# One tiled MoE kernel: gating between the decoding operations, a third attention tile moved ahead, a spare accumulator bank

## The chip, the core and the metric

The kernel runs on one core of a Trainium2 chip. The metric is device time in microseconds (us) of one execution, smaller is better. TensorE (PE in the rows, with PEld for its weight loads) does the matmuls and transposes, VectorE (DVE) and ScalarE (ACT) the element-wise work, GpSimd (POOL) the rest, and SyncE's queue (SP, SPq) issues the transfers. Each engine takes its own instructions in the order in which they were written.

## The reference, cut to what matters

Three layers follow each other on 3072 tokens of 512 features:

```
# attention in chunks of 32 rows, over 8 memory rows and a window of 56 keys
a = exp(scale * q_c @ k_full.T - max);  out = (a / sum(a)) @ v_full
# first MoE layer: dense, 512 -> 2048 -> 512
h = x @ w_in;  g = h * clip(h + 3, 0, 6) / 6;  x2 = g @ w_out
# second MoE layer: 8 experts, each token goes to one
idx = argmax(normalised(x2) @ normalised(expert_emb).T / tau)
out[mask] = gate[mask] * (relu(x2[mask] @ w1[e]) @ w2[e])
```

The weights `w_in` and `w_out` arrive in 64 bits a number and are decoded on the chip to a high and a low part of 32 bits each; each product is made of three matmuls (high by high, high by low, low by high).

## The kernel before, in words

Tokens go in 24 tiles of 128. The first dense layer takes them in eight blocks: block 0 of four tiles, block 1 of two, and six blocks of three. Attention of a tile has six stages, `a` (L182: transposes of k and q, then copies into `qT` and `kt`), `s` (L236: scores, `mx`, exponentials), `n` (L269: sums), `p` (L280: transposes of the probabilities, then `pT`), `v` (L294: times v, `xo`; it also issues the transfers of v of the tile after the next) and `x` (L182 again: transposes of `xo` into `xh` and `xl`). They run as side work between the matmuls of an earlier block.

Tiles 0 to 3 are done in a prologue. **Phase one** is the first product of block 0: sixteen steps of twelve matmuls (`mm1`, L393), one for each 128 columns of `w_in`, into two PSUM banks `h` in turn. In each step the engines also decode a later slice of the weights (`decode_w`, L354): three operations on DVE (L369, L370, L371), the second and third waiting for the one before, then a cast on ACT (L376) and a subtraction on POOL (L377); the next slice but two is then requested. Then `gate0` (L426) clamps the step's result: ACT makes relu(h + 3) (L429) and DVE takes the minimum with 6 and multiplies by h (L431), which frees the bank `h` for the step after the next. The last two steps keep their result in the two buffers of the tag `dec`, which the decode also uses. Tile 4 is side work here.

**Phase two** is the second product of block 0 (`mm2`, L449): sixteen steps of twelve matmuls of 512 columns, four tiles at once, with the rest of the decoding (fourteen slices of `w_out`), `split_g` (L437 on ACT, L438 on POOL) and tile 5 as side work. A slice decoded in step t is used in step t + 2.

**Blocks 1 to 7** then run both products in one loop of sixteen steps: `mm1` of step f + 1, side functions of slot f, `mm2` of step f. Side work is attention of the three tiles of the next block and the routing of the block before: `evac` (L457, `x2` from the accumulators), `r_t` (L486: transposes of `x2`, then its split in three by ACT and DVE, L504 to L510), `r_l` (L519: logits), `r_ss`, `r_route`, `r_rank` (L570), `r_sel` (L600), `r_list` (L610), `r_exp`, `r_gate`. Which slot each has is written in tables (`RT4`, `RL4`, tuples in the loop). In block 1 the steps are short, since it has two tiles.

PSUM has eight banks: two for `h`, three for `acc`, two for `s` (stages `a`, `s` and `v`), and one named `att`, which stages `p` and `x` and the routing functions `r_t`, `r_l`, `r_rank` and `r_list` share, one after the other. Block 1 uses two of the three `acc` banks.

The order on each engine is that in which the functions are called here; nothing reorders it. After the three blocks the experts run, which the change does not touch.

Of the kernel before, what the change touches and what calls it, by code (L numbers as in the profile page):

```python
# [30 lines left out]
def attn_moe_kernel(ctx, tc, q, k, v, mem_k, mem_v, w_in, w_out, emb, tau, w1, w2, out, dbg=None):  # L31
# [61 lines left out]
    def bank2():  # L93
        if early["on"]:
            early["s"] += 1
            if early["s"] % 2:
                return pps.tile([P, 2, 512], F32, tag="sp", name="sp", bufs=1)
        return ps.tile([P, 2, 512], F32, tag="s", name="s2", bufs=1)
# [252 lines left out]
            nc.sync.dma_start(out=t.rearrange("p n t -> p (n t)"), in_=w_out[f * P:(f + 1) * P, :])  # L351
        raw[n] = t

    def decode_w(n):  # L354

        f = FORD[n]
        t = raw.pop(n)
        if n < KF:
            t = t.rearrange("p c n t -> p (c n) t")
            dst_h, dst_l = w_in_h[:, :, f * P:(f + 1) * P], w_in_l[:, :, f * P:(f + 1) * P]  # L360
        else:
            for hl in range(2):
                if (hl, f // 2) not in wo:
                    wo[hl, f // 2] = pair(hl, f // 2, F32R)
            dst_h, dst_l = (wo[hl, f // 2][:, f % 2, :] for hl in range(2))
        lo, hi = t[:, :, 0], t[:, :, 1]
        d = late["dw"]().bitcast(I32)
        w = sb.tile([P, 512], I32, tag="dec", name="dec", bufs=2)
        nc.vector.tensor_scalar(out=d, in0=hi, scalar1=0x07FFFFFF, scalar2=3, op0=ALU.bitwise_and, op1=ALU.logical_shift_left)  # L369
        nc.vector.scalar_tensor_tensor(out=d, in0=lo, scalar=29, in1=d, op0=ALU.logical_shift_right, op1=ALU.bitwise_or)  # L370
        nc.vector.scalar_tensor_tensor(out=w, in0=hi, scalar=-0x40000000, in1=d, op0=ALU.bitwise_and, op1=ALU.bitwise_or)  # L371
        load_w(n + 3)
        wf = w.bitcast(F32)
        if n < KF:
            wf = wf.rearrange("p (c n) -> p c n", c=KD)
        nc.scalar.copy(out=dst_h, in_=wf)  # L376
        nc.gpsimd.tensor_tensor(out=dst_l, in0=wf, in1=dst_h.bitcast(F32), op=ALU.subtract)  # L377
# [545 lines left out]
    with tc.manual_schedule():  # L923
# [34 lines left out]

        ndec = [0]

        def dec(n=1):
            for _ in range(n):
                if ndec[0] < 2 * KF:
                    decode_w(ndec[0])
                    ndec[0] += 1

        st = [stages(i) for i in range(BS[0] + BS[1])]
        pw = pps.tile([P, 512], F32, name="pw", bufs=1)
        pdw = pps.tile([P, 512], F32, name="pdw", bufs=1)
        late["dw"] = lambda: pdw  # L970
# [64 lines left out]
        late["ps"] = ctx.enter_context(tc.tile_pool(name="ps2", bufs=1, space=PSUM, reuse_waits="tile"))  # L1035
        late["wp"] = ctx.enter_context(tc.tile_pool(name="wp2", bufs=1, reuse_waits="tile"))
        late["dw"] = lambda: bank("acc", 3)
        a4, a5 = (st[BS[0] + n] for n in range(2))
        side = {1: a4[0], 3: a4[1], 4: a4[2], 6: a4[3], 8: a4[4]}
        hp = mm1(0, 0)  # L1040
        for f in range(KF):
            nxt = mm1(0, f + 1) if f + 1 < KF else None
            if f < KF - 1:
                dec()
            gate0(f, hp)
            if f in side:
                side[f]()
            hp = nxt
# [2 lines left out]
        split_g(1, nc.vector)  # L1051
        pdw2 = bank("h", 2)
        late["dw"] = lambda: pdw2
        side = {0: a5[0], 2: a5[1], 3: a5[2], 5: a5[3], 7: a5[4], 9: a5[5]}
        for t in range(KF):
            mm2(0, STEP[t], first=STEP[0], last=STEP[-1])
            if t + 2 < KF:
                split_g(t + 2)
            dec()
            if t in side:  # L1060
                side[t]()
        for bl in range(NB):
            slot, pre_ = {}, {}
            if bl == 0:
                continue
            if bl + 1 < NB:
                for a in range(TB):
                    st = stages(F0[bl + 1] + a)
                    for o, f_ in zip((0, 1, 2, 3, 4, 5), st):
                        slot.setdefault(5 * a + o, []).insert(0, f_)  # L1070
            if bl:
                d = 2 if bl == 1 else 0
                for t in range(BS[bl - 1]):
                    (wt, f), (wl, f2) = (RT4 if bl == 1 else RT)[t], (RL4 if bl == 1 else RL)[t]
                    (pre_, slot)[wt].setdefault(f, []).append(lambda t=t: r_t(bl - 1, t, bank2()[:, 0, :] if bl == NB - 1 else None))
                    (pre_, slot)[wl].setdefault(f2, []).insert(0, lambda t=t: r_l(bl - 1, t))
                    slot.setdefault((8, 8, 9, 9)[t] + d // 2, []).append(lambda t=t: r_ss(bl - 1, t))
                slot.setdefault(8 + d, []).append(lambda: r_route(bl - 1))
                slot.setdefault(9 + d, []).append(lambda: r_rank(bl - 1))
                slot.setdefault(10 + d, []).append(lambda: r_sel(bl - 1))  # L1080
                slot.setdefault(11 + d, []).append(lambda: r_list(bl - 1))
                slot.setdefault(12 + d, []).append(lambda: r_exp(bl - 1))
                slot.setdefault(12 + d, []).append(lambda: r_gate(bl - 1))
                if bl == EB + 1:
                    slot.setdefault(12, []).append(pick_first)
                    slot.setdefault(14, []).append(pick_rest)
            if bl == NB - 1:
                at_ctx.close()
                p2["pool"] = ctx.enter_context(tc.tile_pool(name="p2", bufs=1, side="right", reuse_waits="tile"))
                for n in range(NE):  # L1090
                    load_x(("E", n))
                eE = [nc.values_load(e0i[0:1, n:n + 1], engines=[SP], min_val=0, max_val=E - 1) for n in range(2)]
                todo = [(st, p, i) for p in range(4) for st in range(2) for i in range(2)]
                rws = {}

                def pre(n=1):
                    for _ in range(n):
                        if todo:
                            st, p, i = todo.pop(0)
                            rws[st, p, i] = load_half(p, i, eE[st])  # L1100

                def go(st, p, i, eng=None):
                    split_half(st, p, i, rws.pop((st, p, i)), eng)
                    pre()

                pre(RW)
                for n, f in enumerate(SP_):
                    slot.setdefault(f, []).append(lambda n=n: go(n // 2 % 2, n // 4, n % 2, nc.gpsimd if n in PG else None))
                slot.setdefault(1, []).append(plan_const)
                slot.setdefault(13, []).append(lambda: T_x(("E", 0)))  # L1110
            mm1(bl, 0)
            if bl:
                evac(bl - 1)
            for f in range(KF):
                for g_ in pre_.get(f, []):
                    g_()
                if f + 1 < KF:
                    mm1(bl, f + 1)
                for g_ in slot.get(f, []):
                    g_()  # L1120
                if bl < NB - 1 or f < KF - 1:
                    mm2(bl, f)
# [147 lines left out]
```

## Time and profile before

| | |
|---|---|
| median of 3 runs | 1080.92 us (1080.29 to 1081.65) |
| the profiled execution | 1078.23 us, of which the span from first to last instruction 1076.4 us |
| PE busy | 1019.2 us, 95% of the span |
| DVE, ACT, POOL busy | 521.8, 430.6, 153.1 us |
| mean granted TensorE clock | 0.981 of 2.4 GHz |

PE's busy time in 40 equal slices, in tenths, reads `8877898889999999999999999998999999999994`: PE has idle time in the first quarter of the span and little behind it. The first quarter holds the prologue (to about 44 us), phase one (44 to 117 us), phase two (117 to 168 us) and block 1 (168 to 245 us). A stretch in which PE waits is read from what ended the wait; a stretch in which another engine is busy matters only where PE waits for it.

### The profile page before, as it was taken

How to read it: one execution, taken by the hardware profiler on the slowest of the kernel's cores; microseconds unless marked ns; L12 is line 12 of the kernel's file. 1: busy time of each engine (PE TensorE's matmuls, PEld its weight loads, DVE VectorE, ACT ScalarE, POOL GpSimd, SP SyncE). 2: the span in 40 equal slices, each digit the busy share in tenths (PEclk: the TensorE clock that was granted, in tenths of full speed). 3: DMA queues.
4: the chain of work that ended last, by engine and by line, in shares of the span. 5: the costliest groups of instructions: out<-in, count | busy, mean ns of one | idle time of the engine just before them, and what ended most of it. 6: DMA issues, size and time to landing. Idle time of an engine off the chain costs nothing.

```text
span 1076.4 us, 22714 instructions
## 1 busy us (share of the span) xinstructions
PE 1019.2 (95%) x8350; PEld 860.2 (80%) x8350; DVE 521.8 (48%) x1194; ACT 430.6 (40%) x769; POOL 153.1 (14%) x155
## 2 busy tenths in 40 slices
PE   8877898889999999999999999998999999999994
PEld 5555676778888888888888888886888888888883
DVE  5656774454454554554554454666124333326530
ACT  5332443333433433433433433663234444436531
POOL 1222581000000000000000001033111122112210
PEclk9889999999999999999999999998999999999997
DMA  8744440114121121121121103341133514337610
GB/s 190 163 120 153 131 164 21 38 40 74 38 60 38 39 75 30 38 70 39 38 71 34 28 31 126 110 127 47 53 109 112 190 47 130 121 119 245 217 50 22
DMA packets 133914, 95.50 MB, mean 89 GB/s; under 512 B 100789, under 2 KB 109013, under 8 KB 133792
## 3 DMA queue, kind: packets, MB, share of 16 engines
q1 hardware_dynamic: 129184, 80.51, 26.8%
q0 software_dynamic: 4448, 13.42, 3.9%
q8 instruction: 67, 1.10, 0.4%
q14 instruction: 55, 0.45, 0.1%
q10 hardware_dynamic: 160, 0.02, 0.0%
HBM read 156.83 MB, written 13.38 MB: 158 GB/s over the span
## 4 chain that ended last, share of the span: by engine, by line
PE 80%; DVE 7%; issue 4%; ACT 3%; DMA 2%; SPq 1%; POOL 1%; POOLq 0%; DVEq 0%; ACTq 0%
PE h L393 22%; PE acc L449 21%; PE acc L797 12%; PE h L766 12%; PE s L775 2%; PE s L182 2%; PE s L236 1%; PE s L294 1%; PE att L748 1%; DVE dec L371 1%; PE att L182 1%; PE att L486 1%; DMA out_dram<-r,m_tid 1%; PE att L280 1%; PE att L519 1%
## 5 line engine op out<-in xcount | busy, mean ns | idle before, releaser
L449 PE MATMUL acc<-wo,gh 128*128 128x512 f32 x640 | 207.1, 405 | 0.2 <-ACT x L468 0.2
L393 PE MATMUL h<-xh,w_in_h 128*128 128x384 f32 (+2 forms) x512 | 177.7, 347 | 17.0 <-DVE wo L431 11.1
L393 PE MATMUL h<-xl,w_in_h 128*128 128x384 f32 (+2 forms) x512 | 175.2, 342 | 0.1
L393 PE MATMUL h<-xh,w_in_l 128*128 128x384 f32 (+2 forms) x512 | 174.6, 341 | 0.0
L406 ACT ACTIVATE g<-h,three 128x384 f32<-128x384 f32 (+1 forms) x112 | 63.6, 567 | 176.8 <-PE h L393 176.3
L407 DVE SCALAR_TENSOR_TENSOR g<-g,h 128x384 f32<-128x384 f32 (+1 forms) x112 | 59.7, 533 | 152.7 <-ACT g L406 152.5
L449 PEld LDWEIGHTS acc<-wo,gh 128*128 128x128 f32 x640 | 113.3, 189 | 19.7 <-ACT x L468 0.5
L449 PE MATMUL acc<-wo,gl 128*128 128x512 f32 x320 | 126.4, 395 | 0.0
L393 PEld LDWEIGHTS h<-xh,w_in_h 128*128 128x128 f32 x512 | 98.0, 191 | 28.7 <-DVE wo L431 14.5
L393 PEld LDWEIGHTS h<-xl,w_in_h 128*128 128x128 f32 x512 | 97.6, 191 | 7.5 <-DVE xl L331 1.0
L393 PEld LDWEIGHTS h<-xh,w_in_l 128*128 128x128 f32 x512 | 97.8, 191 | 3.2
L402 DVE TENSOR_TENSOR gl<-g,gh 128x384 fp32r<-128x384 f32 (+1 forms) x112 | 60.9, 544 | 63.2 <-ACT gh L401 63.2
L401 ACT CAST gh<-g 128x384 fp32r<-128x384 f32 (+1 forms) x112 | 55.7, 498 | 73.9 <-DVE g L407 72.7
L536 POOL TENSOR_TENSOR rn_y<-ss,half 128x3 f32<-128x3 f32 (+2 forms) x8 | 6.9, 860 | 474.2 <-ACT junk L526 474.2
L753 DVE TENSOR_TENSOR tl<-att,th 128x512 fp32r<-128x512 f32 x26 | 18.0, 692 | 115.6 <-ACT th L752 109.3
L449 PEld LDWEIGHTS acc<-wo,gl 128*128 128x128 f32 x320 | 60.2, 188 | 14.0 <-DVE gl L402 0.3
L734 POOL DMA_INDIRECT xg<-xb,m_ix x27 | 27.9, 1032 | 259.6 <-PE h L766 210.4
L797 PE MATMUL acc<-wo,th 128*128 128x512 f32 x192 | 60.6, 397 | 0.0
L752 ACT CAST th<-att 128x512 fp32r<-128x512 f32 x26 | 15.2, 586 | 106.9 <-PE acc L797 105.2
L769 ACT ACTIVATE hs<-h 128x512 f32<-128x512 f32 x54 | 32.2, 598 | 64.2 <-PE h L766 60.3
L797 PE MATMUL acc<-w_in_h,th 128*128 128x512 f32 x120 | 49.4, 412 | 0.0
L766 PE MATMUL h<-wo,th 128*128 128x512 f32 x192 | 48.8, 396 | 0.0
(311 smaller groups left out, 1846.3 us busy)
## 6 DMA issues: line engine op xcount, KB each, us to landing
rw<-in_moe_w_dram SPq DMA_DIRECT2D x136, 512.0 KB
vw<-in_v_dram SPq DMA_DIRECT2D x176, 56.0 KB
raw_in<-in_moe_w_in_dram SPq DMA_DIRECT2D x16, 512.0 KB
raw_out<-in_moe_w_out_dram SPq DMA_DIRECT2D x16, 512.0 KB
k_t<-in_k_dram SPq DMA_DIRECT2D x24, 256.0 KB
q_t<-in_q_dram SPq DMA_DIRECT2D x24, 256.0 KB
xb<-x SPq DMA_DIRECT2D x20, 256.5 KB
xb<-x SPq DMA_DIRECT2D x4, 256.0 KB
```

The costliest lines, as they stand in the source:

```text
L182: nc.tensor.transpose(dst[:, j * P:(j + 1) * P], t[:, 2 * j:2 * j + 2, :].rearrange("p a d -> p (a d)"), ident)
L393: nc.tensor.matmul(hp, lhsT=wt[:, c, f * P:(f + 1) * P], rhs=xc, start=(n == 0), stop=(n == 3 * KD - 1))
L401: nc.scalar.copy(out=gh, in_=g)
L402: nc.vector.tensor_tensor(out=gl, in0=g, in1=gh.bitcast(F32), op=ALU.subtract)
L406: nc.scalar.activation(out=g, in_=hp, func=AF.Relu, bias=three)
L407: nc.vector.scalar_tensor_tensor(out=g, in0=g, scalar=6.0, in1=hp, op0=ALU.min, op1=ALU.mult)
L449: nc.tensor.matmul(acc[bl][t], lhsT=gt[:, t * P:(t + 1) * P], rhs=wo[hl, f // 2][:, f % 2, :], start=(f == first and n == 0), stop=(f == l ...
L734: nc.gpsimd.indirect_dma_start(out=t[:, :], out_offset=None, in_=src, in_offset=bass.IndirectOffsetOnAxis(ap=ix[:, 0:1], axis=0), bounds_c ...
L766: nc.tensor.matmul(hp, lhsT=a[:, kk, :], rhs=wpart(st, hl, p, kk), start=(kk == 0 and a is th and hl == 0), stop=(kk == KD - 1 and a is tl))
L769: nc.scalar.activation(out=h_t[n][:, p, :], in_=hp_t.pop((n, p)), func=AF.Relu)
L775: nc.tensor.transpose(hp[:, j * P:(j + 1) * P], h[:, j * P:(j + 1) * P], ident)
L797: nc.tensor.matmul(o, lhsT=a[:, KD + f, :], rhs=wpart(st, hl, 2 + half, kk), start=(f == 0 and c == 0), stop=(f == KE - 1 and c == 2))
```

## The change

Three edits, all of them about order and about one bank:

- `decode_w` takes a function `first` and calls it between its first and its second DVE operation. In phase one, `gate0` of the step is handed in, so that relu and gate stand ahead of the second and third decoding operation, the cast and the subtraction. The last step has no decode and calls `gate0` alone.
- Attention of tile 6, the first of block 2, moves from block 1 to phase two, except its stage `x`, which stays in block 1, in slot 0. Three stages of tile 5 move up by one step for it. In block 1 the two tiles that are left get other slots.
- In block 1, `r_t` writes into the third `acc` bank (`late["px"]`), taken once for all four tiles, in place of `att`.

```diff
-    def decode_w(n):
+    def decode_w(n, first=None):
 ...
         nc.vector.tensor_scalar(out=d, in0=hi, scalar1=0x07FFFFFF, scalar2=3, op0=ALU.bitwise_and, op1=ALU.logical_shift_left)
+        if first:
+            first()
         nc.vector.scalar_tensor_tensor(out=d, in0=lo, scalar=29, in1=d, op0=ALU.logical_shift_right, op1=ALU.bitwise_or)
 ...
             if f < KF - 1:
-                dec()
-            gate0(f, hp)
+                dec(1, lambda: gate0(f, hp))
+            else:
+                gate0(f, hp)
 ...
-        side = {0: a5[0], 2: a5[1], 3: a5[2], 5: a5[3], 7: a5[4], 9: a5[5]}
+        side = {0: a5[0], 2: a5[1], 3: a5[2], 4: a5[3], 6: a5[4], 8: a5[5], 9: a6[0], 10: a6[1], 12: a6[2], 13: a6[3], 15: a6[4]}
 ...
+        def spare(bl):
+
+            if bl == NB - 1:
+                return bank2()[:, 0, :]
+            if bl == 1 and "px" not in late:
+                late["px"] = bank("acc", 3)
+            return late["px"] if bl == 1 else None
 ...
-                for a in range(TB):
+                if bl == 1:
+                    slot[0] = [a6[5]]
+                for a in range(bl == 1, TB):
                     st = stages(F0[bl + 1] + a)
-                    for o, f_ in zip((0, 1, 2, 3, 4, 5), st):
-                        slot.setdefault(5 * a + o, []).insert(0, f_)
+                    for o, f_ in zip((0, 2, 3, 4, 6, 7) if bl == 1 else (0, 1, 2, 3, 4, 5), st):
+                        slot.setdefault((1, 8)[a - 1] + o if bl == 1 else 5 * a + o, []).insert(0, f_)
 ...
-                    (pre_, slot)[wt].setdefault(f, []).append(lambda t=t: r_t(bl - 1, t, bank2()[:, 0, :] if bl == NB - 1 else None))
+                    (pre_, slot)[wt].setdefault(f, []).append(lambda t=t: r_t(bl - 1, t, spare(bl)))
```

What stands on DVE in phase one, before, in the third step of sixteen. `wo` at L431 is the gated result, `acc` the decode's scratch bank, `kt` the copies of stage `a` of tile 4; the rows start with the gate of the second step:

```order
L431 SCALAR_TENSOR_TENSOR wo_844<-wo_844,h_822 128x512
L197 COPY kt<-s_871 128x4x3x16
L201 COPY kt<-s_871 128x4x3x8
L204 COPY kt<-s_871 128x4x8
L369 TENSOR_SCALAR acc<-raw_in 128x512
L370 SCALAR_TENSOR_TENSOR acc<-raw_in,acc 128x512
L371 SCALAR_TENSOR_TENSOR dec<-raw_in,acc 128x512
L431 SCALAR_TENSOR_TENSOR wo_912<-wo_912,h_847 128x512
```

And now (the added lines move the line numbers by two: the gate is L433, the second and third decoding operation L372 and L373); the rows start with the first decoding operation of the second step:

```order
L369 TENSOR_SCALAR acc<-raw_in 128x512
L433 SCALAR_TENSOR_TENSOR wo_838<-wo_838,h_822 128x512
L372 SCALAR_TENSOR_TENSOR acc<-raw_in,acc 128x512
L373 SCALAR_TENSOR_TENSOR dec<-raw_in,acc 128x512
L197 COPY kt<-s_871 128x4x3x16
L201 COPY kt<-s_871 128x4x3x8
L204 COPY kt<-s_871 128x4x8
L369 TENSOR_SCALAR acc<-raw_in 128x512
L433 SCALAR_TENSOR_TENSOR wo_906<-wo_906,h_847 128x512
```

The gate stands behind the first decoding operation instead of behind the third, and the copies of stage `a` come behind two decoding operations more.

On DVE in phase two, around the ninth step, before: two steps' decoding with stage `x` of tile 5 (`xl`) between them.

```order
L371 SCALAR_TENSOR_TENSOR dec<-raw_out,h_1339 128x512
L331 TENSOR_TENSOR xl<-att,xh 128x4x128
L369 TENSOR_SCALAR h_1339<-raw_out 128x512
L370 SCALAR_TENSOR_TENSOR h_1339<-raw_out,h_1339 128x512
L371 SCALAR_TENSOR_TENSOR dec<-raw_out,h_1339 128x512
L369 TENSOR_SCALAR h_1339<-raw_out 128x512
```

Now, from the decode of the tenth step on: `kt` and the rows at L244 to L253 are stages `a` and `s` of tile 6.

```order
L373 SCALAR_TENSOR_TENSOR dec<-raw_out,h_1339 128x512
L197 COPY kt<-s_1702 128x4x3x16
L200 COPY kt<-s_1702 128x4x16
L201 COPY kt<-s_1702 128x4x3x8
L204 COPY kt<-s_1702 128x4x8
L369 TENSOR_SCALAR h_1339<-raw_out 128x512
L372 SCALAR_TENSOR_TENSOR h_1339<-raw_out,h_1339 128x512
L373 SCALAR_TENSOR_TENSOR dec<-raw_out,h_1339 128x512
L244 MEMSET s_1747 32x2x4x16
L248 TENSOR_REDUCE mx<-s_1747 128x8
L253 TENSOR_TENSOR e<-s_1747,mx 128x2x4x64
L369 TENSOR_SCALAR h_1339<-raw_out 128x512
```

Seven operations of tile 6, the first and the fifth of which need results of PE, stand between decodes that had one operation between them.

On PE in block 1, before, in slot 3: the transposes of stage `p` and behind them `r_t` of the second tile, both into `att`.

```order
L393 MATMUL h_2013<-xh,w_in_l 128x256
L280 MATMUL att<-ident,e 128x128 x4
L486 MATMUL att<-ident,x_1836 128x128 x4
L449 MATMUL acc<-wo_1424,gh 128x512
L449 MATMUL acc<-wo_1425,gh 128x512
L449 MATMUL acc<-wo_1424,gl 128x512
```

Now the same pair stands in slot 5, with stage `p` of another tile and `r_t` of the third:

```order
L395 MATMUL h_2210<-xh,w_in_l 128x256
L280 MATMUL att<-ident,e 128x128 x4
L488 MATMUL acc<-ident,x_1951 128x128 x4
L451 MATMUL acc<-wo_1513,gh 128x512
L451 MATMUL acc<-wo_1514,gh 128x512
L451 MATMUL acc<-wo_1513,gl 128x512
```

`r_t` names `acc` as its target now; stage `p` still writes into `att`, which ACT then copies out.

## Rows read from the trace of the kernel before

**Rows 1.** windows: length, busy us of PE, PEld, DVE, ACT, POOL; PEclk, DMA, GB/s

```profile
49.00:117.00 68.00, 52.02 (x326) 38.59 (x325) 42.46 (x69) 23.47 (x46) 18.21 (x15) 0.95 0.44 132
117.00:168.00 51.00, 50.13 (x336) 38.99 (x336) 34.61 (x54) 19.80 (x36) 37.63 (x34) 0.97 0.42 135
168.00:245.00 77.00, 63.92 (x812) 55.48 (x811) 39.22 (x116) 29.89 (x66) 1.05 (x1) 0.98 0.18 40
...
172.00:176.00 4.00, 3.71 (x26) 3.48 (x27) 1.68 (x4) 1.72 (x5) 0.00 (x0) 1.00 0.12 28
236.00:240.00 4.00, 4.00 (x39) 3.48 (x45) 0.00 (x0) 0.07 (x1) 0.00 (x0) 0.57 0.00 0
```

**Rows 2.** timeline, a phase-one step: start us, us, engine, line, operation [idle before <-releaser]

```profile
76.20 0.69 DVE L431 SCALAR_TENSOR_TENSOR wo<-wo,h 128x512 f32<-128x512 f32 x1 [1.27 <-ACT wo L429]
76.81 0.69 DVE L369 TENSOR_SCALAR acc<-raw_in 128x512 int32<-128x512 int32 x1
...
77.53 0.69 DVE L370 SCALAR_TENSOR_TENSOR acc<-raw_in,acc 128x512 int32<-128x512 int32 x1
...
78.33 0.69 DVE L371 SCALAR_TENSOR_TENSOR dec<-raw_in,acc 128x512 int32<-128x512 int32 x1
...
79.05 0.62 ACT L376 CAST w_in_h<-dec 128x512 fp32r<-128x512 f32 x1 [2.88 <-DVE dec L371]
...
79.58 0.68 ACT L429 ACTIVATE wo<-h,three 128x512 f32<-128x512 f32 x1
...
79.75 1.28 POOL L377 TENSOR_TENSOR w_in_l<-dec,w_in_h 128x512 fp32r<-128x512 f32 x1 [2.81 <-ACT w_in_h L376]
...
80.29 0.69 DVE L431 SCALAR_TENSOR_TENSOR wo<-wo,h 128x512 f32<-128x512 f32 x1 [1.28 <-ACT wo L429]
```

**Rows 3.** timeline of DVE: first and fifteenth gate of phase one (sixteen in all)

```profile
49.89 0.69 DVE L431 SCALAR_TENSOR_TENSOR wo<-wo,h 128x512 f32<-128x512 f32 x1 [2.94 <-ACT wo L429]
...
114.08 0.69 DVE L431 SCALAR_TENSOR_TENSOR g<-g,h 128x512 f32<-128x512 f32 x1 [1.28 <-ACT g L429]
```

**Rows 4.** timeline of ACT: the eight exponentials of the side tile in phase one

```profile
67.73 1.75 ACT L261 ACTIVATE e<-s,mx 128x64 f32<-128x64 f32 x8 [2.86 <-DVE mx L248]
```

**Rows 5.** timeline: the passage from phase one to phase two

```profile
113.54 1.27 POOL L377 TENSOR_TENSOR wo<-dec,wo 128x512 fp32r<-128x512 f32 x1 [3.04 <-ACT wo L376]
...
114.85 0.69 ACT L429 ACTIVATE g<-h,three 128x512 f32<-128x512 f32 x1 [0.80 <-POOL wo L377]
...
116.58 1.22 PE L449 MATMUL acc<-wo,xh 128*128 128x512 f32 x2 [2.28 <-ACT xh L437]
```

**Rows 6.** chain of waits, merged: start us, us, what; side stages; six mm2 twice

```profile
173.92 0.87 PE s L182 x8
174.79 1.38 PE acc L449 x6
...
191.78 0.79 PE s L294 x53
...
212.42 0.63 PE att L280 x4
...
235.54 2.11 PE acc L449 x6
```

**Rows 7.** waits of PE, 168 to 245 us: total us, times, longest us

```profile
PE att L610 <- ACT pT L282: 3.2, 1, 3.2
PE h L393 <- DVE x L466: 2.6, 1, 2.6
PE att L486 <- DVE xl L331: 2.5, 1, 2.5
PE att L280 <- DVE x2T L510: 1.8, 1, 1.8
PE att L519 <- DVE x2T L510: 1.3, 1, 1.3
PE att L486 <- ACT pT L282: 1.0, 1, 1.0
```

More of the change, by code (lines that the diff above doesn't have):

```diff
@@ L959, in attn_moe_kernel, with dec @@
         ndec = [0]
-        def dec(n=1):
+        def dec(n=1, first=None):
             for _ in range(n):
                 if ndec[0] < 2 * KF:
-                    decode_w(ndec[0])
+                    decode_w(ndec[0], first)
                     ndec[0] += 1
-        st = [stages(i) for i in range(BS[0] + BS[1])]
+                elif first:
+                    first()
+        st = [stages(i) for i in range(BS[0] + BS[1] + 1)]
         pw = pps.tile([P, 512], F32, name="pw", bufs=1)
@@ L1037, in attn_moe_kernel @@
         late["dw"] = lambda: bank("acc", 3)
-        a4, a5 = (st[BS[0] + n] for n in range(2))
+        a4, a5, a6 = (st[BS[0] + n] for n in range(3))
         side = {1: a4[0], 3: a4[1], 4: a4[2], 6: a4[3], 8: a4[4]}
```

## The prediction

> **What bounds the kernel now.** I read the windows first. PE is at work nearly all the time from block 2 on; what can still be won or lost lies in the three stretches that the change touches. In phase one (49 to 117 us) PE is busy 52.0 of 68.0 us, in phase two 50.1 of 51.0, in block 1 63.9 of 77.0 [rows 1]. So phase two is PE's, and the other two have 16 and 13 us of idle PE.
>
> Phase one next, in the timeline of one step. The gate at 76.20 is followed by the three decoding operations at 76.81, 77.53 and 78.33, the cast at 79.05, the relu at 79.58 and the next gate at 80.29 [rows 2]: 4.09 us, in which each instruction starts when the one before has ended, on DVE and ACT in turn. PE, with twelve matmuls (2.8 us: twice the 1.38 us of six in [rows 6]), only follows. That is the bound of phase one: a ring through DVE and ACT, because the relu of a step stands behind the cast of its decode.
>
> Block 1 last, in PE's waits: six of 1.0 to 3.2 us, together 12.4 us. Four of them (3.2, 2.5, 1.8, 1.0) end when somebody has emptied `att`, the bank that routing and attention share [rows 7].
>
> **Phase one, the ring.** Nothing is added; gate and relu move. The new order is decode 1, gate, decode 2, decode 3, cast, relu of the next step. The ring then goes gate to decode 2 (0.61, as gate to decode 1 now), decode 2 to 3 (0.80), to the cast (0.72), to the relu (0.53), to the gate (0.71) [rows 2]: 3.37 us. Decode 1 (0.72 of the 4.09) drops out, since DVE does it while ACT is at the cast and the relu (1.24 us). There are 14 intervals from the first gate to the fifteenth: 14 x 0.72 = **10.1 us less**. PE's 2.8 us still fit into 3.37. What is late next: the decoded low part. Today POOL starts 0.70 behind the cast and takes 1.28; in the new order that ends at 0.61 + 0.80 + 0.72 + 0.70 + 1.28 = 4.1 us behind the gate, and the step that uses it starts a second gate later (3.37) plus some 0.7 us for PE to take up the freed bank: 4.1, and its low part is needed only by the third matmul. It just fits.
>
> The 14 intervals take 114.08 - 49.89 = 64.2 us now [rows 3], 14 x 4.09 = 57.3 of them the ring; 6.9 us come from the side stages of tile 4. After the change DVE operations of the side that ended the wait alone hide behind cast and relu; the eight exponentials, 1.75 us on ACT [rows 4], and the wait for the transposes stay. Bounds are 1.75 and 6.9; I take 4.5, nearer to the middle: **2.4 us less**.
>
> **Phase one, its end.** The last gate writes into the buffer that the last decode used, so its relu waits for POOL: 114.85, right behind POOL's 113.54 + 1.27 [rows 5]. Today that decode stands ahead of the fifteenth gate, and the relu comes 0.77 behind it. In the new order the gate (0.61), decode 2 (0.80), decode 3 (0.72), and the cast up to POOL's start (0.70) and POOL (1.27) all follow the fifteenth gate: 4.1 us. The first matmul of phase two, 1.73 behind that relu [rows 5], so comes 5.9 us behind the fifteenth gate and not 2.5: **3.4 us more**. Together phase one ends 10.1 + 2.4 - 3.4 = 9.1 us earlier, at about 107.5.
>
> **Phase two.** Stages `a`, `s`, `p` and `v` of tile 6 come in: 0.87, 0.79 (as for `v`), 0.63 and 0.79 us of PE [rows 6], 3.1 us, in a stretch that has no idle PE: **3.1 us more**. Their DVE work now stands among the decodes, and both `kt` and `mx` must wait for PE, with the decodes of three steps queued behind them and POOL and PE behind those. From a decode's first operation to POOL's end is 79.75 + 1.28 - 76.81 = 4.2 us [rows 2], and a slice has two steps of 2.8 us from decode to use: 1.4 us are spare, against the `kt` and `mx`/`e` work of some 2 us behind PE's end of a stage. Bounds: 0 and 3 us; I take **0.5 us more**, because tile 5 goes through the same stages there today and PE is busy 50.1 of 51.0 us. The transfers of `vw` for tile 8 and of k and q move with the stages. Only the last request of `w_out` stands behind k and q on SP's queue, three steps ahead of its use; I cost that at nothing, and it is in the 3 us if that cover is gone. ACT's part (two copies, an exponential, one copy) fits beside its 19.8 busy of 51 us [rows 1].
>
> **Block 1.** It loses the same four stages: **3.1 us less**. Of its waits [rows 7]: the 2.6 behind `evac` stays, nothing moves there. The 1.8 and 1.0 and the 2.5 of `r_t` and `p` on `att` go, since `r_t` has a bank of its own. The 1.3 of `r_l` stays, because one `r_l` still stands two slots behind a slot with `s` and `r_t`. In place of the 2.5, the last `r_l` now needs `att` from stage `x` of tile 7 in the slot ahead, with one `mm2` (1.4 us) between: 1.1 remain. The 3.2 of `r_list` came from `pT` queued on ACT behind DVE's `r_sel` in the slot ahead; `p` is a slot earlier now, and what is left is `r_sel` itself, about 0.9. `r_rank` stands behind `s` of tile 8, where it stood behind stage `x`: 0.7 new. That leaves 2.6 + 1.3 + 1.1 + 0.9 + 0.7 = 6.6 of 12.4: **5.8 us less**; bounds 3 and 9.
>
> **The clock.** Behind the 3.2 us wait the granted clock is 0.57 in 236 to 240 us, that is partly the lower level of 1.2 GHz [rows 1], and six matmuls take 2.11 and not 1.38 us [rows 6]; `mm2` and `mm1` of a step pay about **1.5 us**, which go if that gap goes. Behind the 2.6 us wait that ended at 172.29 the clock stayed at 1.00 [rows 1]. The Trainium skill says in "TensorE: Matmul & The Clock Gate", section "Part 1: The HAM clock gate", that "the default state is throttled, and activity releases the throttle". By that alone each gap of some us would bring the lower level, the 2.6 us one too, and the longer gap at the end of phase one, and the sum would be 1.5 to 3 us worse; the 1.00 in the row says that the gap's length alone does not decide.
>
> **The sum.** -9.1 + 3.1 + 0.5 - 3.1 - 5.8 - 1.5 = -15.9 us. Against the profiled execution's own 1078.23 us this gives 1062.3; that execution ran 2.7 us under the median of the runs, 1080.92, so against the median 1065.0. About 0.2% (2.2 us) is what a measurement of this kernel can tell from no change.
>
> **Rivals.**
> 1. *The third tile starves the decode.* `kt` and `mx` hold DVE until PE is through with a stage, and three decodes come late in a row, each costing PE up to 1 us; the 3 us bound and the low block 1 bound together: 1065 + 2.5 + 2.8 = about 1070. For it: three steps in a row have DVE work that waits for PE. Against: tile 5 does it already.
> 2. *The passage and the clock take it back.* PE's gap at the end of phase one, 2.3 us now [rows 5], grows by up to the 3.4 us above; if a slow stretch follows in phase two and the one in block 1 stays, 1.5 us each: 1068.
> 3. *The ring does not open.* If the second decoding operation starts no earlier than now, because it still waits for its own engine, the 10.1 us stay away: 1075. Against: decode 2 needs only decode 1 and the data, and DVE idles 1.27 us ahead of each gate [rows 2].
> 4. *Slower: PE at the lower level in phase one.* At 1.2 GHz twelve matmuls take 5.6 us, above the ring's 3.37, and PE sets the step: 2.2 us more each. From 8 of the 15 steps on this eats the 15.9 us; with all, 1065 + 33 = 1098. Against: the clock in phase one is 0.95 with more idle PE than there will be [rows 1].
>
> **Chances.** As worked out (1060 to 1068) 0.62; rival 1 0.14; rival 2 0.12; rival 3 0.05; better still, with the tile costing nothing in phase two and less than 4 us of waits in block 1 (below 1060) 0.03; slower, rival 4, 0.04. The predicted time is 1065. Rivals 1 and 2 lie inside a range that goes to 1072; below, the bounds of block 1 and of the side stages reach 1059. Rivals 3 and 4 are left out. Faster by over 0.2% are all but rival 4 and a little of rival 3: 0.95; within 0.2% 0.01; slower 0.04.
>
> **What would show it.** Gates of phase one 3.4 us apart, where 4.09 stood; the last relu some 4 us behind the fifteenth gate with POOL as what ended its wait; the first `mm2` at about 107.5; about 55 us from there to block 1's first matmul; PE's waits on `att` for `r_t` gone, one of about 1 us for the last `r_l`, under 1 us for `r_list`; block 1 about 66 us long; a granted clock of 1.00 late in block 1; all behind it shifted and not changed. The forecast falls if the gates stay 4.1 us apart, if PE waits for POOL's `wo` by more than 3 us in phase two, or if later blocks change their length.

## The result and the profile after

The changed kernel takes **1063.78 us** (median; 1062.72 to 1066.91) where the kernel before takes 1081.29 (1080.29 to 1081.98): a ratio of 0.984, with a 95% interval of 0.982 to 0.987. The forecast was 1065.0 us, 1059 to 1072. The profiled execution that is read here took 1062.98 us, its span is 1061.2; beside the one of before (1078.23) that is 15.25 us less.

The windows answer to [rows 1]; the first three lines are phase one, phase two and block 1, the last two are block 1 behind the wait of 2.6 us, and the place where before has its slow stretch. (Length, busy us of PE, PEld, DVE, ACT, POOL; granted clock, DMA, GB/s.)

```profile
49.00:108.00 59.00, 47.94 (x324) 35.76 (x323) 42.15 (x71) 23.38 (x47) 19.61 (x16) 0.98 0.50 152
108.00:163.00 55.00, 53.52 (x453) 41.75 (x455) 37.61 (x64) 21.94 (x40) 37.82 (x34) 0.96 0.43 135
163.00:229.00 66.00, 59.91 (x708) 51.71 (x701) 35.87 (x106) 27.44 (x62) 1.05 (x1) 1.00 0.17 38
168.00:172.00 4.00, 4.00 (x31) 3.74 (x31) 1.68 (x4) 1.37 (x3) 0.00 (x0) 1.00 0.07 16
236.00:240.00 4.00, 4.00 (x84) 3.52 (x83) 1.99 (x7) 2.06 (x4) 0.00 (x0) 1.00 1.06 110
```

Phase one is 9 us shorter with nearly the same work of DVE in it (42.15 us; 42.46 before): what left is idle time. Phase two is 4 us longer, block 1 11 us shorter, and 0.57 at 236 to 240 us has become 1.00.

One step of phase one, from the timelines of DVE and ACT (start us, us, operation, [idle before <- releaser]), answers to [rows 2]:

```profile
76.83 0.69 DVE L433 SCALAR_TENSOR_TENSOR wo<-wo,h 128x512 f32<-128x512 f32 x1 [1.16 <-ACT wo L431]
77.44 0.69 DVE L372 SCALAR_TENSOR_TENSOR acc<-raw_in,acc 128x512 int32<-128x512 int32 x1
78.23 0.69 DVE L373 SCALAR_TENSOR_TENSOR dec<-raw_in,acc 128x512 int32<-128x512 int32 x1
78.83 0.69 DVE L369 TENSOR_SCALAR acc<-raw_in 128x512 int32<-128x512 int32 x1
80.19 0.69 DVE L433 SCALAR_TENSOR_TENSOR wo<-wo,h 128x512 f32<-128x512 f32 x1 [0.67 <-ACT wo L431]
...
78.95 0.62 ACT L378 CAST w_in_h<-dec 128x512 fp32r<-128x512 f32 x1 [2.15 <-DVE dec L373]
79.48 0.69 ACT L431 ACTIVATE wo<-h,three 128x512 f32<-128x512 f32 x1
```

The gates are 3.36 us apart where they were 4.09. Decode 1 (L369) at 78.83 now runs while ACT is at the cast and the relu; that is all that happened to the step.

The end of phase one, from the timelines of DVE, ACT, POOL and PE, answers to [rows 5]:

```profile
101.86 0.69 DVE L433 SCALAR_TENSOR_TENSOR g<-g,h 128x512 f32<-128x512 f32 x1 [0.67 <-ACT g L431]
...
104.67 1.26 POOL L379 TENSOR_TENSOR wo<-dec,wo 128x512 fp32r<-128x512 f32 x1 [2.06 <-ACT wo L378]
...
105.97 0.69 ACT L431 ACTIVATE g<-h,three 128x512 f32<-128x512 f32 x1 [1.37 <-POOL wo L379]
...
107.70 1.22 PE L451 MATMUL acc<-wo,xh 128*128 128x512 f32 x2 [4.88 <-ACT xh L439]
```

The fifteenth gate is at 101.86; the last relu waits for POOL until 105.97, and PE stands for 4.88 us, where it stood for 2.28.

PE's waits in block 1 (160 to 230 us; total us, times, longest) answer to [rows 7]:

```profile
PE h L395 <- DVE x L468: 2.6, 1, 2.6
PE att L521 <- DVE xl L331: 1.2, 1, 1.2
PE att L521 <- DVE x2T L512: 0.6, 1, 0.6
PE att L572 <- DVE r_oh L560: 0.5, 1, 0.5
PE att L280 <- DVE lg L524: 0.4, 1, 0.4
PE att L280 <- DVE r_eq L581: 0.3, 1, 0.3
PE att L521 <- ACT x L510: 0.2, 1, 0.2
```

Of 12.4 us in six large waits 5.8 us in smaller ones are left; `r_list` and `r_t` wait no more. Only the 2.6 us behind `evac` is what it was.

### The profile page after: what moved, and what is told of

The parts are those of the page before. It is cut to its first block, busy times and chain, and to the rows that moved or that the text cites. A ratio compares the mean times of both kernels' runs of the same rounds, so it can differ in the third digit from the quotient of the medians.

```text
span 1061.2 us, 22705 instructions
## 1 busy us (share of the span) xinstructions
PE 1013.5 (96%) x8350; PEld 855.5 (81%) x8350; DVE 519.3 (49%) x1194; ACT 429.4 (40%) x769; POOL 153.4 (14%) x155
## 4 chain that ended last, share of the span: by engine, by line
PE 78%; DVE 7%; issue 5%; ACT 3%; DMA 2%; POOL 1%; SPq 1%; POOLq 0%; DVEq 0%; ACTq 0%
PE acc L451 22%; PE h L395 20%; PE acc L799 12%; PE h L768 12%; PE s L777 2%; PE s L182 2%; PE s L294 1%; PE s L236 1%; DVE dec L373 1%; PE att L750 1%; PE att L280 1%; PE att L182 1%; DMA out_dram<-r,m_tid 1%; DMA raw_in<-in_moe_w_in_dram 1%; PE att L488 1%
## 5 line engine op out<-in xcount | busy, mean ns | idle before, releaser
L409 DVE SCALAR_TENSOR_TENSOR g<-g,h 128x384 f32<-128x384 f32 (+1 forms) x112 | 59.7, 533 | 143.5 <-ACT g L408 143.4
L404 DVE TENSOR_TENSOR gl<-g,gh 128x384 fp32r<-128x384 f32 (+1 forms) x112 | 60.8, 543 | 63.2 <-ACT gh L403 63.2
```

What stands on the lines that cost most here:

```text
L404: nc.vector.tensor_tensor(out=gl, in0=g, in1=gh.bitcast(F32), op=ALU.subtract)
L409: nc.vector.scalar_tensor_tensor(out=g, in0=g, scalar=6.0, in1=hp, op0=ALU.min, op1=ALU.mult)
```

## The experiments

Each kernel was set against the kernel before on the same chip, whose median was 1079.18 beside E1 to E4, 1079.79 beside E5 to E8 and 1080.96 us beside E9 to E11. The table has the starts of three instructions, from each kernel's timeline of PE, as lengths of the stages: first gate to first `mm2` (phase one), from there to block 1's first matmul (phase two), from there to block 2's first (block 1). Medians of different groups stand beside different befores, so they are compared by their ratios; where those intervals overlap, the stage lengths of the profiled executions say more.

| kernel | median us | ratio to before (95%) | phase one | phase two | block 1 |
|---|---|---|---|---|---|
| before | 1081.29 | | 66.69 | 51.59 | 76.12 |
| after | 1063.78 | 0.9844 (0.9820 to 0.9867) | 58.35 | 55.67 | 65.04 |
| E1 gate alone | 1071.58 | 0.9935 (0.9915 to 0.9954) | 58.45 | 53.27 | 76.24 |
| E2 tile and bank alone | 1072.27 | 0.9944 (0.9925 to 0.9963) | 66.63 | 55.24 | 64.98 |
| E3 after, no bank | 1064.59 | 0.9884 (0.9854 to 0.9913) | 58.28 | 55.82 | 66.26 |
| E4 after, gate first | 1074.89 | 0.9954 (0.9933 to 0.9975) | 67.38 | 56.30 | 66.55 |
| E5 after, gate later | 1060.31 | 0.9802 (0.9764 to 0.9841) | 53.21 | 56.43 | 66.52 |
| E6 after, old last step | 1063.81 | 0.9839 (0.9800 to 0.9877) | 57.22 | 55.36 | 64.96 |
| E7 after, loads apart | 1065.51 | 0.9856 (0.9810 to 0.9901) | 57.29 | 56.17 | 66.36 |
| E8 E5, E6 and E7 | 1057.93 | 0.9798 (0.9750 to 0.9847) | 50.59 | 54.30 | 65.00 |
| E9 after, h carried out first | 1062.17 | 0.9841 (0.9816 to 0.9865) | 58.88 | 56.27 | 62.68 |
| E10 E8 and E9 | 1054.98 | 0.9771 (0.9756 to 0.9785) | 50.61 | 55.87 | 62.69 |
| E11 after once more | 1065.88 | 0.9862 (0.9845 to 0.9880) | 57.95 | 56.60 | 66.66 |

**E1 and E2, the two halves.** E1 is the kernel before with the first edit (`decode_w`, `dec` and the loop of phase one), E2 the changed kernel without it.

> The kernel before with the gate between the decoding operations and nothing else. By the theory of the sum (phase one 8.9 us shorter as the trace of after has it, the rest as before, less 0.5 to 1.5 us because the longer gap of PE at the passage brings a longer slow stretch): 8.9 - 1 = about 8 us less than before, 1073.4 us against 1081.3. First mm2 at about 107.7; gates 3.36 us apart; block 1 with its waits of before (3.2, 2.5, 1.8, 1.0 us on att) and its slow stretch. Rival: the parts are not independent, and the shorter phase one is worth something only with the third tile moved (its decodes and transfers run closer together in either case); then less than 6 us.

> The change without the gate: the third tile's stages in phase two and the bank for x2. By the sum: phase two 3.6 to 4.2 us longer, block 1 some 11 us shorter with the slow stretch at 236 to 240 us gone, so 7 to 7.5 us less than before, about 1074. Phase one as before (gates 4.09 apart, first mm2 at 116.6). With e1 the two parts should add to the 17.5 us of the whole change within 1.5 us. Rival: what block 1 gained is owed to another clock history (the slow stretch merely moved to the passage), and without the gate the slow stretch stays in block 1: then 5.5 us or less, with a granted clock under 0.8 behind a wait in block 1.

E1 came out 7.6 us under the before of its chip, E2 6.9 us. That is 14.5 us together, and the expectation was 17.5 within 1.5: by the medians it failed. But the whole change was worth 17.5 us on one chip and 15.1 on another (E11), so the medians do not settle it, and the profiles have to. At block 2's first matmul E1's profile is 7.1 us ahead of before and E2's 7.5, together 14.6; after is 15.9 ahead. So the halves add, to 1.2 us, and neither needs the other. A good part of the 1.2 us is a wait that only E1 has: late in its phase two PE waits 0.85 us for POOL's `wo`, because DVE waited 2.02 us for `raw_out` (1.00 in before), whose request stands behind sixteen loads of v on SP's queue. In after, phase one has such a wait (E7). E1 keeps every wait of [rows 7] and its slow stretch in block 1 (76.24 us). E2 keeps phase one, and its block 1 is that of after while at the passage the clock fell for no longer than in before: the rival of E2, a slow stretch that only moved, is out. PE's two other waits for POOL's `wo` in phase two are 0.20 and 0.25 us in before and in E1, and 0.57 and 0.65 in E2, as in after (0.58 and 0.65), so their growth comes with the third tile and not with the gate.

**E3, what the bank is worth.**

```diff
-  ... r_t(bl - 1, t, spare(bl))
+  ... r_t(bl - 1, t, bank2()[:, 0, :] if bl == NB - 1 else None)
```

> The changed kernel with the transposes of x2 in block 1 back in att, the stages where the change puts them. Theory: the moved stages have taken most of the waits away by themselves; the bank saves the two places where something that empties att stands one slot ahead of r_t, stage x (about 1.1 us, as the last r_l waits for it in after) and stage p (1.0 us as before): 2 us slower than after, 1065.8. Bounds 1 and 3.5. Rival: the bank itself is most of the 7 us that the waits of block 1 fell by: 5 us or more slower than after.

The three longest waits of PE for `att` in block 1 of E3:

```profile
PE att L521 <- DVE xl L331: 1.2, 1, 1.2
PE att L521 <- DVE x2T L512: 1.1, 1, 1.1
PE att L488 <- ACT pT L282: 1.0, 1, 1.0
```

One `r_t` waits again, for stage `p` (1.0); the other place, behind stage `x`, does not show. Block 1 is 1.2 us longer (66.26), within the bounds of the expectation and far from the rival's 5 us. The median is 0.8 us longer (by the ratios 4 us, with intervals that overlap), which the runs cannot tell from nothing. All of PE's waits in block 1 are 7.1 us in E3, where before has 12.4 and after 5.8: most of them went because the stages moved, and beside the moved stages the bank is the smallest of the three edits. What it would be worth without them, no run shows.

**E4, the gate still earlier.** Both the ring and an earlier release of `h` would explain the gain; this order parts them.

```diff
-        nc.vector.tensor_scalar(out=d, in0=hi, scalar1=0x07FFFFFF, ...)
         if first:
             first()
+        nc.vector.tensor_scalar(out=d, in0=hi, scalar1=0x07FFFFFF, ...)
```

> The changed kernel with the gate ahead of all three decoding operations, so that it is earlier than in either kernel. Theory (a ring through DVE and ACT, whose length depends on what stands between the gate and the cast): the cast stands behind all three again, and the interval goes back to 4.09 us; 14 intervals 10.2 us longer, the end of phase one 0.7 us longer, so 1063.8 + 11 = about 1075. Rival: the change gains because the gate gives the bank h back to PE earlier, ahead of the decode; then this order is as good or better: 3.4 us or less, 1064 or less.

A step of E4, timeline of DVE (the gate is L433, decode 1 to 3 are L371 to L373):

```profile
71.20 0.69 DVE L433 SCALAR_TENSOR_TENSOR wo<-wo,h 128x512 f32<-128x512 f32 x1 [0.24 <-ACT wo L431]
71.80 0.69 DVE L371 TENSOR_SCALAR acc<-raw_in 128x512 int32<-128x512 int32 x1
...
73.33 0.69 DVE L373 SCALAR_TENSOR_TENSOR dec<-raw_in,acc 128x512 int32<-128x512 int32 x1
75.29 0.69 DVE L433 SCALAR_TENSOR_TENSOR wo<-wo,h 128x512 f32<-128x512 f32 x1 [1.28 <-ACT wo L431]
```

4.09 us again, with the old wait of 1.28 us ahead of the gate; the rival, 1064 us or less, is out. That the median is 1074.89, where 1075 was expected, is partly luck. Phase one is 9.0 us longer than in after, not 11: the 14 intervals took 60.72 us, 8.2 more and not 10.2, because what comes on top of the plain steps is 3.5 us here and not 5.5. The rest is 0.6 us in phase two and 1.5 in block 1, where the clock fell (last section). What counts is how many operations stand between the gate and the cast, not how early the gate is.

**E5, the gate one operation later.** `first()` now stands between the second and the third decoding operation.

> The changed kernel with the gate one operation later, between the second and the third decoding operation. By the ring theory only decode 3, cast and relu stand between two gates: 0.61 + 0.72 + 0.53 + 0.71 = 2.6 us, less than PE's twelve matmuls, so PE sets the step at 2.8 to 2.9 us: 14 x 0.5 = 7 us less; POOL ends 3.3 and not 4.1 us behind the fifteenth gate, 0.8 less; the wait for raw_in grows by some 2 us, since three steps now last 8.4 us: 1063.8 - 6 = about 1058. Rival: what the change won is that one operation overlaps cast and relu, which last 1.24 us and have no room for two (1.5 us); then nothing more comes of it, and the later release of h costs up to 0.6 us a step: 1063 to 1072.

Timeline of DVE in E5 (decode 3 is L373, decode 1 L369, decode 2 L370):

```profile
84.64 0.69 DVE L433 SCALAR_TENSOR_TENSOR wo<-wo,h 128x512 f32<-128x512 f32 x1
85.25 0.68 DVE L373 SCALAR_TENSOR_TENSOR dec<-raw_in,acc 128x512 int32<-128x512 int32 x1
85.84 0.69 DVE L369 TENSOR_SCALAR acc<-raw_in 128x512 int32<-128x512 int32 x1
86.56 0.70 DVE L370 SCALAR_TENSOR_TENSOR acc<-raw_in,acc 128x512 int32<-128x512 int32 x1
87.20 0.69 DVE L433 SCALAR_TENSOR_TENSOR wo<-wo,h 128x512 f32<-128x512 f32 x1
```

Between these gates the step is 2.56 us, and DVE has no idle time in it. The kernel cannot keep that up, though: PE starts a matmul every 0.233 us (twelve take 2.80 us, 84.32 to 87.12), and has no idle time either. The window from 82 to 90 us (length, then busy us of PE and the others, as above), and the second gate of phase one on DVE:

```profile
82.00:90.00 8.00, 8.00 (x36) 6.31 (x35) 6.41 (x11) 3.78 (x7) 3.37 (x3) 1.00 0.54 143
...
52.16 0.69 DVE L433 SCALAR_TENSOR_TENSOR wo<-wo,h 128x512 f32<-128x512 f32 x1 [0.18 <-ACT wo L431]
```

The first interval, which has no side stage in it, is 2.81 us (49.35 to 52.16). In it DVE waits for the relu, and the relu starts 0.76 us behind the cast instead of 0.52, 2.80 us behind the relu of the step before. So PE sets the step, as expected; 2.56 us are DVE's own four operations, seen where DVE catches up behind a side stage. The 14 intervals took 47.99 us, 4.5 less than after (52.51), where 5 were expected (7 for the steps, less 2 for `raw_in`). The wait for `raw_in` hardly grew (2.13 us; 1.90 in after), but side stages and that wait cost 8.8 us beside steps of 2.80, where they cost 5.5 beside steps of 3.36; that fits a PE with no idle time left to hide them in, and no run parts it further. Phase one is 5.1 us shorter. Of these 2.2 us are lost again: phase two is 0.8 longer, and block 1 1.5, because the clock fell behind the wait of 2.57 us (last section). The median is 3.5 us under that of after, with ratios whose intervals overlap; the rival, that two operations do not fit behind cast and relu, is out.

**E6, the last step as it was.**

```diff
-            if f < KF - 1:
+            if f < KF - 2:
                 dec(1, lambda: gate0(f, hp))
             else:
+                dec(KF - 1 - f)
                 gate0(f, hp)
```

> The changed kernel with the last decode of phase one whole ahead of the fifteenth gate, as in the kernel before; all other steps as changed. If the chain gate, decode 2, decode 3, cast, POOL, last relu is what ends phase one, the last relu follows 0.8 us behind the fifteenth gate and not 4.1, that gate comes 0.7 later, and mm2 begins 2.7 us earlier, behind a gap of PE of some 2.3 and not 4.9 us; the slow stretch at the passage then is 3.4 and not 6.8 us long, worth another 1 to 1.7 us: 1063.8 - 4 = about 1060. Rival: the slow stretch follows from the work of PE in the steps before and not from that gap; then it stays as long and only 2.7 us come: 1061.1.

This expectation failed. The end behaves as told: the last gate is 1.48 us behind the fifteenth. But the interval ahead of it grew to 5.55 us, in the timeline of DVE:

```profile
99.58 0.56 DVE L433 SCALAR_TENSOR_TENSOR g<-g,h 128x384 f32<-128x384 f32 x1 [0.82 <-ACT g0r L431]
...
100.25 0.69 DVE L372 SCALAR_TENSOR_TENSOR acc<-raw_out,acc 128x512 int32<-128x512 int32 x1
101.05 0.69 DVE L373 SCALAR_TENSOR_TENSOR dec<-raw_out,acc 128x512 int32<-128x512 int32 x1
101.65 0.69 DVE L369 TENSOR_SCALAR acc<-raw_out 128x512 int32<-128x512 int32 x1
...
103.17 0.69 DVE L373 SCALAR_TENSOR_TENSOR dec<-raw_out,acc 128x512 int32<-128x512 int32 x1
105.13 0.69 DVE L433 SCALAR_TENSOR_TENSOR g<-g,h 128x512 f32<-128x512 f32 x1 [1.27 <-ACT g L431]
```

At the step where the order changes back, the rest of one decode and a whole one stand between two gates; the expectation had counted only decode 1 (0.7 us), not the 2.2 us that it is. Phase one won 1.1 us instead of 2.7 (PE's gap is 3.65 us, not 2.3), and the median is that of after. The slow stretch at the passage is 3.4 us long again, so the rival, that it stays as long, is out; but phase two is only 0.3 us shorter and not 1 to 1.7, because much of after's longer stretch lies where PE has no work ("The clock", below). The 3.4 us at the end are the price of the order, not a slip in it.

**E7, the loads apart.** One thing in after's phase one was not foreseen: an interval of 4.59 us (gates at 90.28 and 94.87), in which DVE waits 1.90 us for `raw_in`. SP's queue in after says why:

```profile
82.31 0.37 SPq L345 DMA_DIRECT2D raw_in<-in_moe_w_in_dram  x1
82.85 3.90 SPq L167 DMA_DIRECT2D vw<-in_mem_v_dram  x8
86.80 3.37 SPq L157 DMA_DIRECT2D vw<-in_v_dram  x8
90.26 0.39 SPq L345 DMA_DIRECT2D raw_in<-in_moe_w_in_dram  x1
```

The request stands behind sixteen loads, which take 7.3 us to issue, about two of the new steps. E7 moves eight of them two slots on.

```diff
                     load_mv(i + 2)
-                    load_v(i + 2)
+                    if i != BS[0]:
+                        load_v(i + 2)
...
-        side = {1: a4[0], 3: a4[1], 4: a4[2], 6: a4[3], 8: a4[4]}
+        side = {1: a4[0], 3: a4[1], 4: a4[2], 6: a4[3], 8: a4[4], 10: lambda: load_v(BS[0] + 2)}
```

> The changed kernel with the eight loads of v for tile 6 two steps later than the eight of mem_v, so that SP's queue does not hold sixteen in a row ahead of a request of raw_in. If that queue is what made the thirteenth interval 4.6 and not 3.5 us, DVE's wait for raw_in (1.9 us) goes and the kernel is 1.1 us faster: 1062.7. Rival: the transfer itself is late because the loads share the DMA engines; then the wait stays, or moves by two steps, and the time is 1063.8.

DVE does not wait for `raw_in` any more, the three intervals from the twelfth gate on take 10.51 and not 11.58 us, and phase one is 1.06 us shorter, as told; the rival, a wait that stays or moves, is out. The time does not show it (1065.51 us, from 1062.64 to 1067.94): block 1 is 1.3 us longer behind the same slow stretch as in E5.

**E8, E5 to E7 together.**

> The three edits of the other runs of this group together: gate between the second and the third decoding operation, last decode of phase one ahead of the fifteenth gate, loads of v apart. If they add: -7 (intervals of 2.8 to 2.9 us), -1.1 (raw_in), -2.7 to -4 (passage): about 1052. Rival: with PE as the bound of phase one, the gains share what PE leaves, and phase two gives back what its decode cannot follow (POOL's waits there, 1.2 us, grow): 1056 or more.

Phase one is 7.8 us shorter than in after; E5, E6 and E7 have 5.1, 1.1 and 1.1 by themselves, so the gains add. PE's two waits for POOL's `wo` in phase two did not grow (0.59 and 0.65 us), but a wait of 0.62 us for POOL's `xl` (L440) is new. Phase two is 1.4 us shorter, and that is the clock of this execution: E10, the same kernel up to block 1, takes 55.87 us there and not 54.30. Windows of E8 and then of E10, behind the first `mm2` (at 99.65 and 99.02):

```profile
101.00:104.00 3.00, 2.99 (x16) 2.52 (x17) 2.49 (x4) 0.56 (x2) 0.00 (x0) 1.00 0.00 0
```

```profile
101.00:104.00 3.00, 3.00 (x9) 2.32 (x8) 1.85 (x3) 0.00 (x0) 0.00 (x0) 0.50 0.02 5
```

The profiled execution has a span of 1052.6 us; the median, 1057.93 (1054.32 to 1063.89), lies higher than the 1052 of the expectation and is wide.

**E9, E10 and E11: the wait that the change left.** Behind phase two PE waits 2.57 us for the second bank of `h`, which holds the fourth result. Timeline of DVE in after (L409 and L404 are the gate and the low part of block 1's first step, L468 carries the result out):

```profile
165.63 0.42 DVE L409 SCALAR_TENSOR_TENSOR g<-g,h 128x256 f32<-128x256 f32 x1 [1.35 <-ACT g L408]
166.52 0.42 DVE L404 TENSOR_TENSOR gl<-g,gh 128x256 fp32r<-128x256 f32 x1 [0.47 <-ACT gh L403]
166.87 0.68 DVE L468 TENSOR_SCALAR x<-h 128x512 f32<-128x512 f32 x1
```

The result has been ready since PE's last `mm2` of phase two (162.26 us), but the instruction stands behind a gate that waits for PE.

```diff
+            if bl == 1:
+                evac(0, [3])
             mm1(bl, 0)
             if bl:
-                evac(bl - 1)
+                evac(bl - 1, [2, 1, 0] if bl == 1 else None)
```

> The changed kernel with one edit in block 1, a place that the change left alone: the fourth result of phase two, which lies in the second bank of h, is carried out ahead of the first gate of block 1 and not behind it. The 2.57 us in which PE waits ahead of its second step for that bank then go; the first mm2 of block 1 may wait up to 1 us for the other banks: 1.6 to 2.6 us less than after, about 1061.7. A slow stretch of the clock behind that place, which came in three of the other profiled kernels and not in after, must not come. Rival: the wait only moves to the mm2 of the step, whose banks are carried out at the same time as before: 1063.5.

> All four edits together: gate between the second and the third decoding operation, last decode of phase one whole ahead of the fifteenth gate, loads of v apart, and the fourth result of phase two carried out first. If the last one is worth beside the others what it is worth alone: 2 us under the three together, a span of about 1050.6 us where those had 1052.6 and after 1061.2; median about 1054. Rival: phase one now ends so early that another wait comes in: no better than the three together, 1052.6 us of span.

> The changed kernel itself once more, on the same chip and in the same rounds as the two runs beside it, so that they can be set against it: 0.982 to 0.987 of before.

The wait is gone in E9 and E10, no other grew, and block 1 takes 62.7 us where E11 and after have 66.66 and 65.04: 2.4 us for the wait, and where the clock falls behind it, 1.6 more. E9 takes 1062.17 us (1061.7 expected) beside the 1065.88 of E11; the intervals overlap, so what the edit is worth is read from the trace and not from the time. E10's span, 1048.6 us, lies under the 1050.6 expected, and its median near the 1054. E11 came out as expected (0.986). E10 takes 1054.98 us beside the 1065.88 of E11 on the same chip; the intervals, 0.976 to 0.979 and 0.985 to 0.988 of before, lie apart. So **E10 beats both kernels**, by 26 and 11 us.

## Why the prediction was right, step by step

| step of the prediction | forecast us | measured us |
|---|---|---|
| plain interval of phase one | 3.37 | 3.36 |
| first gate | 0 | -0.5 (49.35; 49.89 before) |
| 14 intervals, ring | -10.1 | -10.2 (14 x 0.73) |
| 14 intervals, side stages | -2.4 | -1.5 |
| end of phase one | +3.4 | +3.3 (fifteenth gate to `mm2` 5.84; 2.50 before) |
| first `mm2` | 107.5 | 107.70 |
| phase two | +3.6 | +4.1 |
| block 1 | -10.4 | -11.1 |
| sum at block 2 | -15.9 | -15.9 (228.41; 244.29 before) |

- **The ring** was the bound, and its length could be added up from five rows of before. E4 gives the same rule another length (4.09, as added up). E5 does not test it: the rule's 2.6 us lies under PE's 2.80, which sets the step there.
- **The side stages.** The intervals' excess over the ring fell from 6.9 to 5.5 us. The -2.4 us were there, but the wait for `raw_in`, 1.07 us by E7, came on top. The prediction named SP's queue in phase two and found it harmless; in phase one, where steps became shorter than what the queue had to issue, it did not look. Nor do the 6.9 us follow from the step's length: E4, with steps of 4.09 us too, has 3.5. Its order and its granted clock (1.00 all through phase one) both differ from before's, and no run parts the two.
- **The end** came as told, through the buffer of the last gate and POOL.
- **Phase two** is 0.5 us over the forecast. PE's waits for POOL grew by 0.8 us (from 0.4 to 1.2), against the 0.5 taken; the longer slow stretch is an estimated 0.5 ("The clock", below). That leaves 2.8 for the stages of tile 6, where 3.1 were forecast; no run parts these.
- **Block 1.** Its waits fell to 5.8 us; 6.6 were forecast. By name: the last `r_l` 1.2 (1.1 forecast), the other `r_l` 0.8 in two parts (1.3), `r_rank` 0.5 (0.7), `evac` 2.6 (2.6); `r_list` none (0.9); 0.7 in two small waits of `p` (L280) were not named. The reason given was right only in part. The prediction let the waits of `r_t` and `p` (2.5, 1.8 and 1.0) go because `r_t` has a bank of its own; in E3, without that bank, only the 1.0 comes back, and 0.3 at `r_l`. The other two went with the stages that moved. The number was right and its cause, for the larger part, was not the one named.
- **The clock.** The stretch at 236 to 240 us went with the wait ahead of it. But the one at the passage grew; that is rival 2, in part, and it stood in no term of the sum. Windows of before from its first `mm2`, and of after ahead of its first `mm2` and from it (the granted clock is the number ahead of the last two):

```profile
116.58:119.58 3.00, 2.87 (x6) 1.86 (x7) 2.74 (x4) 0.47 (x1) 1.27 (x1) 0.50 0.00 0
```

```profile
105.70:107.70 2.00, 0.00 (x1) 0.00 (x1) 1.01 (x2) 1.73 (x4) 0.23 (x1) 0.50 0.35 131
107.70:111.70 4.00, 3.87 (x8) 2.65 (x9) 3.61 (x5) 0.47 (x1) 1.28 (x1) 0.50 0.00 0
```

By slices of 1 us the lower level lasts 3.4 us in before, behind a gap of PE of 2.3 us, and 6.8 us in after, behind one of 4.9. But 2.5 of the 6.8 us lie in the gap, where PE has nothing to do. Behind the first `mm2` it is 4.3 us instead of 3.4, at half the clock an estimated 0.5 us more. On the other side, phase one of before had slow stretches, too, which after has not (granted clock 0.58 at 62 to 66 and 0.57 at 72 to 76 us in before, 1.00 in both in after); some of what the side stages won may be theirs, and no run parts it.
- **The rivals.** 3 is excluded by the 3.36 us, 4 by the granted clock of phase one, 0.98 and not 0.50; of 1 came 0.8 us. Behind block 2's first matmul after loses 0.6 us of the 15.9 (15.2 less in span). No run here was made to settle that.
- **The chances.** Every large term had a row of its own in the trace of before; the sum was good to a microsecond by parts because the two halves hardly touch each other (E1 and E2), not because errors were absent: +0.9 in the side stages and +0.5 in phase two stand against -0.7 in block 1 and -0.5 ahead of the first gate, where the start-up of the program, which the change does not touch, came out shorter. That these cancel is luck: over the thirteen profiled executions the first gate alone comes between 48.07 and 50.41 us. So is part of the hit itself. In E11, the same kernel, the way from the first gate to block 2 took 181.21 us and not 179.06, because the clock stayed low for longer at the passage and fell behind the 2.6 us wait too, which the prediction had put at nothing.

## What to carry to other kernels

When two engines hand a step to and fro, count the operations between one hand-over and the next: an operation that needs nothing from the other engine belongs into the time in which that engine works, and how many fit there is told by DVE's idle time ahead of the gate, until the next engine sets the step (here PE, at 2.80 us). A shorter step uncovers what was hidden in the longer one, such as a run of load requests on SP's queue, and an order that is changed back for the last step pays for both orders there. An instruction that frees a bank should not stand on its queue behind one that waits for the engine which needs that bank.

## What the runs showed of the hardware that was not expected

**The same wait, two clocks.** After was profiled in two executions, its own and that of E11. In both PE waits 2.57 us ahead of block 1's second step; the windows 165 to 168 and 168 to 171 us are, for after and then for E11:

```profile
165.00:168.00 3.00, 0.42 (x4) 0.40 (x4) 1.90 (x4) 1.86 (x4) 0.00 (x0) 1.00 0.52 118
168.00:171.00 3.00, 3.00 (x22) 2.74 (x22) 0.88 (x3) 1.23 (x3) 0.00 (x0) 1.00 0.10 22
```

```profile
165.00:168.00 3.00, 0.42 (x3) 0.35 (x3) 1.85 (x4) 1.86 (x4) 0.00 (x0) 0.98 0.51 116
168.00:171.00 3.00, 3.00 (x17) 3.00 (x15) 0.24 (x2) 0.47 (x1) 0.00 (x0) 0.50 0.11 24
```

The same program with the same wait goes on at 2.4 GHz in one and at 1.2 GHz in the other. Behind this wait the clock fell in E4, E5, E7 and E11 and not in before, after, E1, E2, E3, E6 and E8; block 1 was 66.4 to 66.7 us with it and 65.0 without it where nothing else differed (after, E2, E4 to E8, E11). Such a wait so carried, in 4 of 11 executions, another 1.5 us beside its own length. At the passage E8 and E10 part in the same way, behind a wait of 2.41 us in both. What decides it in a given execution, no run here shows; with the wait taken out (E9, E10) the clock did not fall there, but two executions cannot tell that from chance. The prediction had set a rule of the Trainium skill ("TensorE: Matmul & The Clock Gate", "Part 1: The HAM clock gate"), that the lower level is the default and activity releases it, against one row of 1.00 behind this wait. That every gap of some us would then bring the lower level was the prediction's own reading; the rule does not say so, and neither after nor E11 speaks against the rule. That the gap's length alone does not decide is borne out, though one row could not show it: in before the clock fell behind 2.28 us at the passage and not behind 2.57 us in block 1, and after and E11 differ at the same wait.

**Two spacings on DVE.** In the step of after shown above, an operation that does not read the result of the one ahead of it starts 0.60 or 0.61 us behind it (77.44, 78.83), one that does 0.79 (78.23), with 0.69 us of busy time each. In E5 only decode 2 reads what the operation ahead of it has written (0.72 us, 85.84 to 86.56), the other three start 0.59 to 0.64 us behind theirs: four operations of 0.68 to 0.70 us take 2.56 us together.
